# A state-space block with a feed-forward layer on one core: where its tiles lie in SBUF

## The chip, the cores and the metric

One Trainium2 chip, one of its cores. The time is microseconds of device time for one execution of the whole program. Five engines matter here: TensorE (PE; its weight loads are listed apart as PEld), VectorE (DVE), ScalarE (ACT), GpSimd (POOL) and SyncE (SP), which issues nearly all DMAs. SBUF is the on-chip memory in which tiles live, 128 partitions wide; a tile has one start address, the same in each partition, and below "address" always means bytes from the start of a partition.

## The reference, cut to what matters

```python
x = A_u                                            # 1 x 2048 x 512
mod = (silu(c) @ w_mod).reshape(1, 6, 1, -1)
sa, ca, ga, sb, cb, gb = (mod[:, i] for i in range(6))
h = layernorm(x) * (1 + ca) + sa
# S4 convolution: a kernel K[d, l] from 512 x 128 complex parameters,
# y = irfft(rfft(h, 2L) * rfft(K, 2L))[:L] + h * Dskip
x = x + ga * s4(h)
h = layernorm(x) * (1 + cb) + sb
r = maximum(h @ w1 + b1, 0) ** 2                   # 512 -> 1792
x = x + gb * (r @ w2 + b2)                         # 1792 -> 512
```

## The kernel before

The program has two halves, and one core runs them one after the other.

The first half, up to about 300 us, is the convolution as a two-stage discrete Fourier transform written as matmuls. The channels go in 8 groups (`NC`) of 64. For each group the layer-normed input is transformed (`u_pieces`: `stage1` and `stage2`), its halves are swapped by two SBUF-to-SBUF DMAs (`swap_piece`, L777), the convolution's kernel is made from tables of exponentials and sines on POOL, ACT and DVE (`kgen_*`, four units of 16 channels a group, `finish`) and transformed with the same two stages, and `product_pieces` multiplies the spectra (L883) and goes one stage back (L892, copied out by L897). `inverse` (L1088) does the last stage. The second half is the feed-forward layer in split float32r products: `split` (L998, L999) makes a rounded high part on ACT and the rest on DVE or POOL, `three` (L1162 to L1166) multiplies by `w1` in a seven-product scheme, `squares` applies the activation, `product2` (L1204 to L1206) multiplies by `w2`, and `scale` and `store` write out.

The order of work on each engine is computed while the program is built: `keep_order` lists the instructions' data dependences, gives each instruction a modelled duration and an urgency from the `HURRY` table, and pins one order per engine. DMAs go out on SP's queue.

What the change touches is where tiles lie. Tiles come from pools that are filled from two sides. From the left, going up, lie the pool `cst` (small constants, `ctile`), then `ua` (`big0`, the 32 KB tile that holds the parameters, later one half of the back-transformed spectra, later the residual rows `x2`), then `ka` (seven 8 KB tiles `xy0` to `xy6` and the 16 KB `t2_sb`). These are called the lower half below. On the right lies `ub` (`big1`, 32 KB, at the very top), and under it `kp`: the constant selector `spread` in slot `mt`, the two 1 KB tiles `ksb`, the tables `k00` and `k01`, and the three factor tiles `k1`, `k2`, `k3`. These are the upper half. Later tiles reuse these slots: the operands `op...` and `opt...` lie in `xy` slots, `t2t` in that of `t2_sb`, `wset`, `w2t`, `more` (and `i2c` before it) and `work` in `k00`/`k01`, `k1`, `k2` and `k3`, and `rw` in that of `big1`.

Each tile takes a whole number of 32-byte slots. A constant of one float, such as `tiny`, or of two, such as `one_row`, therefore takes 32 bytes, and each such slot in `cst` shifts everything of the lower half by 32 bytes:

```python
    tiny = ctile("tiny", [P, 1])
    one_row = ctile("one_row", [P, 2])
```

Within `kp` the first tile asked for has the lowest address, so the order in which the Python code asks for its tiles sets their places. `spread` is asked for before `kf`, `ksb` at L669, the tables at L785 and the factor tiles at L792.

`tiny` is the bias of a Sign activation in `parameters`. `one_row` holds two columns that sum `ident` over its four quarters; two DVE instructions (L655, L656) read them as per-partition scalars.

Three layouts within tiles come up in the prediction. `piece` and `product_piece` step through an `xy` tile in runs of 16 floats, 64 bytes. `x2`, the residual rows in `big0`, has runs of 64 bytes too. The amplitude tiles in `kgen_rl` (L863) have runs of 32 floats, 128 bytes, every 384 bytes.

Of the kernel before, what the change touches and what calls it, by code (L numbers as in the profile page):

```python
# [39 lines left out]
NE = len(E_VALUES)  # L40
NCH = 64
# [314 lines left out]
def tile_adaln_ssm_ffn(  # L356
# [19 lines left out]
    P = 128  # L376
# [10 lines left out]
    def ring(pool, tag, bufs, shape, dt=F32):  # L387

        if tag not in rings:
            rings[tag] = [[pool.tile(shape, dt, name=f"{tag}{i}") for i in range(bufs)], -1]  # L390
        r = rings[tag]
        r[1] += 1
        return r[0][r[1] % bufs]
# [14 lines left out]
    ctile = lambda name, shape, dt=F32: cst.tile(shape, dt, tag=name, name=name)  # L408
# [6 lines left out]
    unmagic = ctile("unmagic", [P, 1])  # L415
    epsb = ctile("epsb", [P, 1])
    halfpi = ctile("halfpi", [P, 1])
    tiny = ctile("tiny", [P, 1])
    cin = ctile("cin", [P, 4])
    ds4 = ctile("ds4", [P, 128])  # L420
    mv1 = ctile("mv1", [P, 16, 2])
# [5 lines left out]
    def held(pool, slot, name, shape, dt=F32):  # L427

        t = pool.tile(shape, dt, tag=slot, name=name)
        slots[t.tensor.name] = slot  # L430
        return t
# [5 lines left out]
    kp = tc.alloc_tile_pool(name="kp", bufs=1, side="right")  # L437
# [9 lines left out]

    def spectrum():
        return spectra.pop(0)

    def runs(xs):
        return xs.rearrange("p d m t -> p (d m t)")
# [12 lines left out]
    def load_parameters(c0, n):  # L465
        nc.sync.dma_start(raw[:, c0 : c0 + n, 0:6], prm[:, c0 : c0 + n])

    heads = [spectrum() for _ in range(4)]
    rows = [runs(t)[:, 512 * i : 512 * i + 512] for t in heads for i in range(4)]
    load_parameters(0, 1)  # L470
# [11 lines left out]
    def wm_next():  # L482
        wms.append(spectrum())
        wm = wms[-1].rearrange("p a b c -> p (a b c)").rearrange("p (a b) -> p a b", a=4)
        wm_load(wm, len(wms) - 1)
        return wm
# [10 lines left out]
    nc.sync.dma_start(ds4, dskip)  # L497
    make_identity(nc, ident)
    by_q = ident.rearrange("p (q a) -> p q a", q=4)
    one_row = ctile("one_row", [P, 2])  # L500
    nc.vector.tensor_reduce(one_row, by_q[:, :, 0:2].rearrange("p q a -> p a q"), axis=mybir.AxisListType.X, op=ALU.add)
    spread = held(kp, "mt", "spread", [P, 128], FR)
    nc.vector.tensor_tensor(
# [162 lines left out]


    whole, in_turn = {}, set()
    scaled = [ring(kp, "ksb", 2, [P, 4, 64]).rearrange("p d x -> p (d x)") for _ in range(2)]  # L669

    def row_pieces():
        for k in range(8):
# [91 lines left out]
    def u_pieces(c):  # L764
        xs = xus[c] = spectrum()
        for g in range(4):
            stage1(x_sb[c][:, 4 * g : 4 * g + 4], xs, 4 * g, evacuate("u", 4 * c + g))
            yield
        for g in range(4):
            evacuate("w", 4 * c + g)(piece(xs, g), stage2(xs, g))  # L770
            yield
# [10 lines left out]
    AHEAD = 1  # L782


    tables = [held(kp, f"k0{i}", f"tables{i}", [P, 2, NCH * NE]) for i in range(2)]  # L785

    def column(t, x):

        o, n, i = (256, 8, 7 - x) if x < 8 else (0, 4, x - 8) if x < 12 else (768, 16, x - 12)
        return t[..., o : o + 64 * n].rearrange("p c (d x) -> p c d x", d=NCH)[..., i]  # L790

    factors = [held(kp, f"k{i}", n, [P, w]) for i, n, w in ((1, "rtl", 3072), (2, "llph", 4096), (3, "rtlph", 4096))]  # L792
    amps = [t[:, 0:3072].rearrange("p (r d x) -> p r d x", r=2, d=16) for t in factors]
    phs = [t[:, 3072:4096] for t in factors[:0:-1]]

# [471 lines left out]
    for k in (0, 2):  # L1267
# [70 lines left out]
        n = uses.index((k + 1, NF - 2))  # L1338
# [38 lines left out]
def build(arrays):  # L1377
    import concourse.bacc as bacc

    nc = bacc.Bacc("TRN2", target_bir_lowering=False, num_devices=1, dynamic_dma_scratch_size=1024)  # L1380
    args = [nc.dram_tensor(n, a.shape, mybir.dt.from_np(a.dtype), kind="ExternalInput").ap() for n, a in arrays.items()]
    args.append(nc.dram_tensor("out_0_dram", (64, 32, 512), F32, kind="ExternalOutput").ap())
    with tile.TileContext(nc, schedule_with_timeline_sim=True) as tc:
        tile_adaln_ssm_ffn(tc, *args)
    return nc
# [12 lines left out]
```

## Time and profile before

| what | value |
|---|---|
| median of 3 runs | 622.15 us |
| the three runs | 621.27, 622.15, 626.71 us |
| time of the profiled execution | 626.13 us |
| its span, first to last instruction | 624.0 us |
| instructions in the profile | 21112 |
| mean granted TensorE clock | 0.982 |
| DMA moved | 57.00 MB, mean 91 GB/s |

The span is what the profile's views divide up; the 2.1 us around it are launch and end. Busy times are sums over an engine's instructions, so engines overlap. In the list of groups each row is a source line, an engine, an operation, the tile written and those read (their numbers left out), the shapes, the count, the busy time and the mean of one. The view of one source line gives the minimum, median and maximum of one instruction in ns, and for a DMA the time from issue to landing in us.

### The profile page before, as it was taken

What the parts mean: (1) busy time and instruction counts of PE and PEld (TensorE: products, weight loads), DVE (VectorE), ACT (ScalarE), POOL (GpSimd) and SP (SyncE); (2) the same over time, 40 slices, a digit from 0 to 9 for tenths busy, and PEclk for the clock granted to TensorE, in tenths of its full rate; (3) what the DMA queues carried; (4) which work ended last, traced back from release to release, by engine and by line L of the source; (5) the groups of instructions that cost most, each with busy time, mean ns of one, the idle gap of its engine ahead of it and who ended that gap; (6) DMA issues with size and microseconds to landing.
All of it is one profiled execution on the core that took longest, in us unless ns stands there. A gap on an engine that the chain in (4) does not pass through costs nothing.

```text
span 624.0 us, 21112 instructions
## 1 busy us (share of the span) xinstructions
PE 565.9 (91%) x9238; PEld 482.1 (77%) x9238; DVE 494.7 (79%) x870; ACT 419.2 (67%) x747; POOL 246.7 (40%) x202
## 2 busy tenths in 40 slices
PE   1258998999999899997799999999999999999996
PEld 1235988899899899986577778787888877778785
DVE  6898988999999899745798997547999876654744
ACT  5688779979967577443576766665766666666540
POOL 5549998999998789270004100000001300000000
PEclk9969999999999999999799999999999999999999
DMA  8905133030311302357008031113522432111431
GB/s 319 409 3 173 37 71 70 4 70 5 70 30 45 70 5 59 99 147 231 4 15 291 19 118 35 34 35 113 176 83 74 146 102 70 36 33 43 142 101 69
DMA packets 31355, 57.00 MB, mean 91 GB/s; under 512 B 4512, under 2 KB 13600, under 8 KB 29856
## 3 DMA queue, kind: packets, MB, share of 16 engines
q1 hardware_dynamic: 30976, 55.53, 29.5%
q8 instruction: 72, 1.18, 0.8%
q14 instruction: 19, 0.16, 0.1%
q10 hardware_dynamic: 288, 0.13, 0.1%
HBM read 43.07 MB, written 4.19 MB: 76 GB/s over the span
## 4 chain that ended last, share of the span: by engine, by line
PE 61%; DVE 17%; ACT 11%; issue 5%; DMA 3%; POOL 1%; DVEq 0%; SPq 0%; ACTq 0%; POOLq 0%
PE ps L892 7%; PE ps L737 6%; PE ps L747 6%; PE kg L873 4%; PE ps L1162 3%; PE ps L1166 3%; PE ps L1164 3%; PE tg L1204 3%; PE tg L1206 3%; PE tg L1205 3%; PE ps L1204 2%; PE ps L1205 2%; PE ps L1206 2%; ACT tables L820 2%; PE tg L1088 2%
## 5 line engine op out<-in xcount | busy, mean ns | idle before, releaser
L1025 POOL TENSOR_TENSOR work<-work 128x256 f32<-128x256 f32 x4 | 3.4, 850 | 199.6 <-DVE t2t L1156 135.7
L999 DVE TENSOR_TENSOR w2t<-rw,w2t 128x512 fp32r<-128x512 f32 x53 | 37.9, 717 | 42.0 <-ACT w2t L998 41.8
L747 PE MATMUL ps<-xy,t_sb 128*64 128x64 f32 x2048 | 65.8, 223 | 1.0 <-DVE xy L883 1.0
L998 ACT CAST w2t<-rw 128x512 fp32r<-128x512 f32 x53 | 32.8, 620 | 48.7 <-PE kg L1206 25.7
L747 PEld LDWEIGHTS ps<-xy,t_sb 128*64 128x64 f32 x2048 | 63.3, 138 | 2.4 <-DVE xy L883 1.2
L892 PE MATMUL ps<-e_sb,xy 128*64 128x128 f32 x1024 | 60.8, 274 | 1.9 <-DVE xy L883 1.2
L892 PEld LDWEIGHTS ps<-e_sb,xy 128*64 128x64 f32 x1024 | 56.1, 138 | 3.2 <-DVE xy L883 1.4
L1149 ACT ACTIVATE more<-more,b1c 128x512 f32<-128x512 f32 x54 | 38.9, 721 | 25.8 <-DVE more L1187 15.9
L1204 PE MATMUL tg<-w2t,t2t 128*128 128x512 f32 x112 | 44.6, 398 | 0.4 <-DVE t2t L1156 0.4
L1206 PE MATMUL tg<-w2t,t2t 128*128 128x512 f32 x112 | 44.3, 396 | 0.0
L1205 PE MATMUL tg<-w2t,t2t 128*128 128x512 f32 x112 | 44.3, 395 | 0.0
L883 DVE TENSOR_TENSOR xy<-ps,xy 128x512 f32<-128x512 f32 x64 | 39.9, 681 | 0.6 <-PE ps L747 0.4
L998 ACT CAST wset<-work 128x512 fp32r<-128x512 f32 (+2 forms) x36 | 24.6, 689 | 22.3 <-DMA work<-w 15.5
L737 PE MATMUL ps<-d_sb,ksb 128*64 128x128 f32 x512 | 33.7, 275 | 3.5 <-issue 2.2
L829 POOL TENSOR_TENSOR rtlph<-lo,big 128x1024 int32<-128x1024 int32 x16 | 34.7, 2168 | 3.0 <-ACT tg L841 2.5
L829 POOL TENSOR_TENSOR llph<-lo,big 128x1024 int32<-128x1024 int32 x16 | 34.3, 2144 | 3.8 <-ACT tg L841 3.6
L1162 PE MATMUL ps<-opt,wset 128*128 128x512 f32 x84 | 33.8, 402 | 1.2 <-ACT more L1173 1.2
L1204 PE MATMUL ps<-w2t,t2t 128*128 128x512 f32 x84 | 33.9, 403 | 0.0
L1205 PE MATMUL ps<-w2t,t2t 128*128 128x512 f32 x84 | 33.2, 396 | 0.0
L1206 PE MATMUL ps<-w2t,t2t 128*128 128x512 f32 x84 | 33.2, 395 | 0.0
L1164 PE MATMUL ps<-opt,wset 128*128 128x512 f32 x84 | 33.1, 394 | 0.0
L737 PE MATMUL ps<-d_sb,big 128*64 128x128 f32 x512 | 32.1, 274 | 0.3 <-ACT big L697 0.2
(287 smaller groups left out, 1637.4 us busy)
## 6 DMA issues: line engine op xcount, KB each, us to landing
rw<-w SPq DMA_DIRECT2D x53, 256.0 KB, 2.7
xy<-xy SPq DMA_DIRECT2D x16, 512.0 KB, 6.3
xy<-xt SPq DMA_DIRECT2D x24, 256.0 KB, 5.2
xy<-w_mod SPq DMA_DIRECT2D x6, 1024.0 KB, 6.4
work<-w SPq DMA_DIRECT2D x12, 512.0 KB, 4.1
out_dram<-more SPq DMA_DIRECT2D x14, 256.0 KB, 2.0
t_sb<-c_t SPq DMA_DIRECT2D x1, 2048.0 KB, 14.8
i2c<-c_i SPq DMA_DIRECT2D x2, 1024.0 KB, 5.2
```

Of the source, the lines that this page charges most:

```text
L737: nc.tensor.matmul(ps[64 * r : 64 * r + 64, 128 * i : 128 * i + 128], src[:, i], d1_sb[:, r], start=True, stop=True)
L747: nc.tensor.matmul(ps[64 * r : 64 * r + 64, 64 * i : 64 * i + 64].rearrange("p (h q t) -> p q h t", h=2, t=2), t2_sb[:, 8 * g + i, r], src ...
L829: nc.gpsimd.tensor_tensor(ph.rearrange("p d r (a b) -> p (d r) a b", a=4), bc(low_phase[:, us].rearrange("p d r b -> p (d r) b"), 2, 4), b ...
L883: nc.vector.tensor_mul(product_piece(y, g), ps, piece(x, g))
L892: nc.tensor.matmul(ps[64 * m : 64 * m + 64, 128 * i : 128 * i + 128], pairs(y)[:, g, i // 2, 64 * m : 64 * m + 64, i % 2], e1_sb[:, h], st ...
L998: nc.scalar.copy(hi_, raw_)
L1149: nc.scalar.activation(c, c if src is None else src, AF.Relu, bias=b1c[:, t : t + 1])
L1162: pe.append(nc.tensor.matmul(ps, dst[:, 0, wi, kt], o[:, 0, kt], start=start and kt == 0, stop=False, skip_group_check=on))
L1164: pe.append(nc.tensor.matmul(ps, dst[:, 1, wi, kt], o[:, 0, kt], start=False, stop=False, skip_group_check=on))
L1204: nc.tensor.matmul(to[m], l[:, xs], hi_, start=(t == 0), stop=False),
L1205: nc.tensor.matmul(to[m], h[:, xs], lo_, start=False, stop=False),
L1206: nc.tensor.matmul(to[m], h[:, xs], hi_, start=False, stop=(t == NF - 1))])
```

## The change

`tiny` becomes a tile of four floats, and `one_row` becomes two of its columns, where it had been a tile of its own. Sixteen bytes still fit into one 32-byte slot, so `cst` has one slot less. The requests for the tables, the factor tiles and the two `ksb` tiles move up to a place ahead of everything else in `kp`. No computing instruction is added, removed or given another shape.

```diff
-    tiny = ctile("tiny", [P, 1])
+    tiny_and_row = ctile("tiny", [P, 4])
+    tiny, one_row = tiny_and_row[:, 0:1], tiny_and_row[:, 1:3]
...
+    tables = [held(kp, f"k0{i}", f"tables{i}", [P, 2, NCH * NE]) for i in range(2)]
+    factors = [held(kp, f"k{i}", n, [P, w]) for i, n, w in ((1, "rtl", 3072), (2, "llph", 4096), (3, "rtlph", 4096))]
+    scaled = [ring(kp, "ksb", 2, [P, 4, 64]).rearrange("p d x -> p (d x)") for _ in range(2)]
...
-    one_row = ctile("one_row", [P, 2])
...
-    scaled = [ring(kp, "ksb", 2, [P, 4, 64]).rearrange("p d x -> p (d x)") for _ in range(2)]
...
-    tables = [held(kp, f"k0{i}", f"tables{i}", [P, 2, NCH * NE]) for i in range(2)]
...
-    factors = [held(kp, f"k{i}", n, [P, w]) for i, n, w in ((1, "rtl", 3072), (2, "llph", 4096), (3, "rtlph", 4096))]
```

The start addresses in the two built programs:

| tile (and who has its slot later) | before | modulo 512 | after | modulo 512 |
|---|---|---|---|---|
| `d1_sb`, `e1_sb`, `ident` | 1152, 2176, 3200 | 128 | the same | 128 |
| `srep`, `gs4`, `g4`, `s4` | 4992 to 6528 | 384 | 32 lower | 352 |
| `lo` | 7680 | 0 | 7648 | 480 |
| `big0` | 11776 | 0 | 11744 | 480 |
| `xy0` to `xy6` (`op...`, `opt...`) | 44544 to 93696 | 0 | 44512 to 93664 | 480 |
| `t2_sb` (`t2t`) | 101888 | 0 | 101856 | 480 |
| `tables0`, `tables1` (`wset0`, `wset1`) | 122848, 137184 | 480 | 120288, 134624 | 480 |
| `rtl`, `llph`, `rtlph` (`w2t`, `i2c`/`more`, `work`) | 151520, 163808, 180192 | 480 | 2560 lower | 480 |
| `ksb0`, `ksb1` | 120800, 121824 | 480 | 194016, 195040 | 480 |
| `spread` (slot `mt`) | 120288 | 480 | 196064 | 480 |
| `big1` (`rw`) | 196576 | 480 | 196576 | 480 |

So the upper half's tiles change places by multiples of 512 bytes, and the lower half's start 32 bytes lower: from a multiple of 512 (and of 64) to 480 modulo 512, which is 224 modulo 256 and 32 modulo 64.

The order of instructions on PE, DVE, ACT, POOL and SP is the same row for row, with the same waits; only names differ. On DVE the rows around the two readers of `one_row`, after the first modulation rows are multiplied, stand before the change as follows (`s` and `s_parts` are the shift row and its rounded part, `big` is `big0`, the numbers behind the names are tiles).

```order
L653 CAST s_parts<-s_306 128x128
L654 TENSOR_TENSOR s_306<-s_306,s_parts 128x128
L655 TENSOR_SCALAR s_306<-s_306,one_row 128x128
L656 SCALAR_TENSOR_TENSOR s_parts<-s_parts,one_row,s_306 128x128
L587 TENSOR_SCALAR big_83<-big_83 128x7x64 x2
```

And after it, on the same engine at the same place:

```order
L657 CAST s_parts<-s_312 128x128
L658 TENSOR_TENSOR s_312<-s_312,s_parts 128x128
L659 TENSOR_SCALAR s_312<-s_312,tiny 128x128
L660 SCALAR_TENSOR_TENSOR s_parts<-s_parts,tiny,s_312 128x128
L591 TENSOR_SCALAR big_83<-big_83 128x7x64 x2
```

Nothing moved: the lines are four lower and `one_row` is now called by the tile that it lies in.

## The prediction

> **What bounds the kernel now.** I read the page first (busy times, the granted clock, the chain of work that ended last), then the groups by shape, then single source lines for the spread of one instruction, then the DMAs' landing times. On the page: the engines' busy shares, the TensorE clock in 40 slices, and the chain by engine.
>
> ```profile
> PE 565.9 (91%) x9238; PEld 482.1 (77%) x9238; DVE 494.7 (79%) x870; ACT 419.2 (67%) x747; POOL 246.7 (40%) x202
> ...
> PEclk9969999999999999999799999999999999999999
> ...
> PE 61%; DVE 17%; ACT 11%; issue 5%; DMA 3%; POOL 1%; DVEq 0%; SPq 0%; ACTq 0%; POOLq 0%
> ```
>
> PE is busy for 91% of the span and holds 61% of the chain; DVE and ACT hold 28% between them, in the places where PE waits for an eviction or a split. DMA holds 3%. In two slices, the third and the twentieth, the clock was below full. The busy time by stretches shows the second of these (columns: stretch, its length, busy time and count of PE, PEld, DVE, ACT and POOL, clock, DMA share, GB/s):
>
> ```profile
> 296.00:304.00 8.00, 5.68 (x171) 4.28 (x171) 4.89 (x17) 2.28 (x5) 0.00 (x0) 0.50 0.02 4
> ```
>
> For at least these 8 us PE ran at half clock, though not full of work. That matters for reading the runs: 5.68 us of PE work at half clock would be 2.84 us at full clock, so a run without this stretch may be some 3 us shorter with the same program. I take this as the likeliest reason, not shown here, why the three runs lie at 621.27, 622.15 and 626.71 us, and the profiled one at 626.13 us, 3.98 above the median.
>
> **What the change removes and adds.** Instructions: none. The order on every engine and every wait is the same, so a cost can only come from an instruction or a transfer that takes another time at another address. The upper half's tiles move by multiples of 512 bytes; the lower half's by 32. So I look for twins: two groups of one shape, one of which before already has the operands' residues modulo 512 that the other will have. The price of an address is then the difference of the two.
>
> *PE.* The first-stage matmul L737 takes weights from `ksb` (480) and streams `d1_sb` (128). L892 takes weights from `xy` (0) and streams `e1_sb` (128). After the change L892 has exactly L737's residues. In the feed-forward layer L1204 to L1206 take weights from `t2t` (0) and stream `w2t` (480), while L1162 to L1166 take them from `wset` (480) and stream `op`/`opt` (0); after, both have 480 on both sides. In the groups by shape:
>
> ```profile
> L892 PE MATMUL ps<-e_sb,xy 128*64 128x128 f32 x1024 | 60.8, 274 | 1.9 <-DVE xy L883 1.2 <-ACT xy L739 0.7
> L892 PEld LDWEIGHTS ps<-e_sb,xy 128*64 128x64 f32 x1024 | 56.1, 138 | 3.2 <-DVE xy L883 1.4 <-ACT xy L739 0.9
> ...
> L1206 PE MATMUL tg<-w2t,t2t 128*128 128x512 f32 x112 | 44.3, 396 | 0.0
> ...
> L737 PE MATMUL ps<-d_sb,ksb 128*64 128x128 f32 x512 | 33.7, 275 | 3.5 <-issue 2.2 <-ACT tg L839 0.8 <-DVE big L897 0.5
> ...
> L1164 PE MATMUL ps<-opt,wset 128*128 128x512 f32 x84 | 33.1, 394 | 0.0
> ...
> L737 PEld LDWEIGHTS ps<-d_sb,ksb 128*64 128x64 f32 x512 | 28.1, 137 | 5.3 <-issue 2.8 <-ACT tg L839 1.0 <-DVE big L897 0.7
> ...
> L1206 PEld LDWEIGHTS tg<-w2t,t2t 128*128 128x128 f32 x112 | 21.0, 188 | 5.1
> ...
> L1164 PEld LDWEIGHTS ps<-opt,wset 128*128 128x128 f32 x84 | 15.8, 188 | 3.4
> ```
>
> 274 against 275, 138 against 137, 396 against 394, 188 against 188 ns: a difference of at most 2 ns, in either direction. The busy time of L892 is 60.8 us for 1024, about 59 ns of PE's time each (274 ns is a latency in a pipeline). One ns on each of the 1024 would be 1.0 us, and that is the bound I carry for L892 from both sides. I take 0, since the twins' weights differ by 1 ns the other way. The second-stage matmuls L747 read `t_sb` and `xy`, both lower, both shifted by the same 32 bytes; they have no twin, and I price them like L892: 0, bound 2.0 us either way (2048 of them).
>
> *DVE and ACT on contiguous tiles.* `split` is the same code on either half:
>
> ```profile
> L739 ACT COPY xy<-ps 128x512 f32<-128x512 f32 x43 | 24.6, 587 | 10.3 <-PE ps L737 10.3
> ...
> L999 DVE TENSOR_TENSOR wset<-work,wset 128x1024 fp32r<-128x1024 f32 x8 | 9.8, 1223 | 3.2 <-ACT wset L998 3.2
> ...
> L999 DVE TENSOR_TENSOR opt<-work,opt 128x1024 fp32r<-128x1024 f32 x8 | 9.6, 1215 | 0.0
> ...
> L697 ACT COPY big<-ps 128x512 f32<-128x512 f32 x16 | 8.9, 587 | 1.9 <-PE ps L691 1.8
> ...
> L999 DVE TENSOR_TENSOR op<-work,op 128x512 fp32r<-128x512 f32 x12 | 7.8, 685 | 0.7 <-ACT op L998 0.7
> ...
> L998 ACT CAST wset<-work 128x512 fp32r<-128x512 f32 x12 | 7.4, 621 | 15.5 <-DMA work<-w 15.5
> ...
> L998 ACT CAST op<-work 128x512 fp32r<-128x512 f32 x12 | 7.0, 622 | 0.1
> ...
> L999 DVE TENSOR_TENSOR wset<-work,wset 128x512 fp32r<-128x512 f32 x8 | 5.5, 686 | 1.8 <-ACT wset L998 1.8
> ```
>
> `op` and `opt` lie low (0) and `work` high (480): mixed residues. `wset` and `work` are both at 480, as all will be. 685 and 686, 1215 and 1223, 622 and 621; and 587 for copies into the lower `xy` and the upper `big1`. With the 8 ns of the 1024 pair as the bound, the 16 mixed instructions here change by 0.1 us. I take 0.
>
> *DVE, ACT and PE on runs of 64 bytes.* L883, L770 and all that works on `x2` step through lower tiles in 64-byte runs that begin at multiples of 64 before, and at 32 modulo 64 after. There is no exact twin. The nearest row is L863, which reads and writes 128-byte runs in upper tiles that begin at 32 modulo 64 (480 + 384 d). A third row is L897, whose 64 copies write 16-byte runs, half into `big0` (0), half into `big1` (480); 38 are on DVE, from both halves. Minimum, median and maximum of one, in ns:
>
> ```profile
> L883 DVE TENSOR_TENSOR xy<-ps,xy x64: 678/680/692, 92.7 to 278.2; 128x512 f32<-128x512 f32 x64
> ...
> L863 DVE SCALAR_TENSOR_TENSOR rtl<-rtl,tg x11: 674/677/687, 53.3 to 245.8; 128x512 f32<-128x512 f32 x11
> ...
> L897 DVE COPY big<-ps x38: 410/415/425, 104.7 to 285.5; 128x256 f32<-128x256 f32 x38
> ```
>
> Runs that begin at 32 modulo 64 cost L863 nothing against L883's aligned ones (677 and 680), nor do 64-byte runs cost L883 anything against the contiguous 685. L897 has one narrow band of 15 ns, with no second group. I take 0. As the upper bound, let each run cost one element more: (1215 - 685) / 512 = 1.04 ns. L883 has 32 runs in and 32 out, 67 ns, times 64 is 4.3 us of DVE; at DVE's 17% of the chain, 0.7 us of the time. Below, nothing: a run cannot be cheaper than the contiguous row shows.
>
> *DMA.* Loads into `xy`, `big0` and `t2_sb` and the swaps now end on addresses at 224 modulo 256. Twins are the loads into upper tiles, which have lain so all along. From the views of single lines (L987 and L478 go to lower tiles, L1043 and L981 to upper ones), and from the waits the one in which PE waits for a lower load:
>
> ```profile
> L987 SPq DMA_DIRECT2D xy<-xt x8: 328/424/987, 277.7 to 281.9; - x8
> ...
> DMA to landing us min/median/max: 2.5/3.9/5.1
> ```
>
> ```profile
> L1043 SPq DMA_DIRECT2D rw<-w x53: 327/328/505, 327.0 to 606.3; - x53
> ...
> DMA to landing us min/median/max: 2.5/2.7/6.2
> ```
>
> ```profile
> L478 SPq DMA_DIRECT2D xy<-w_mod x6: 368/373/379, 14.1 to 59.2; - x6
> ...
> DMA to landing us min/median/max: 4.9/6.4/11.2
> ```
>
> ```profile
> L981 SPq DMA_DIRECT2D i2c<-c_i x2: 327/336/346, 273.6 to 291.5; - x2
> ...
> DMA to landing us min/median/max: 5.1/5.2/5.2
> ```
>
> ```profile
> PE ps L628 <- DMA xy<-w_mod: 1.6, 2, 1.1
> ```
>
> Unqueued, a 256 KB load lands in 2.5 us in either half; a 1 MB load in 4.9 us low and 5.1 us high. So the price is between 0 and 0.2 us a megabyte, and it counts where someone waits: 1.6 us in two waits of PE for `w_mod`. Two loads late by 0.2 us each make 0.4. I take 0.2 us. The swaps L777 shift at both ends, but nothing on DVE is listed as waiting for them.
>
> [...]
>
> *The two readers of `one_row`* and the bias `tiny` read the same number of bytes on the same engines as before: 0.
>
> **The sum:** 0 (PE) + 0 (splits) + 0 (runs) + 0.2 (DMA) = +0.2 us. On the profiled execution 626.13 + 0.2 = 626.3; on the median 622.15 + 0.2 = 622.35, say 622.3 us. The measurement moves by more than this by itself: the three runs span 5.4 us.
>
> **The rivals.**
>
> *Slower, by runs that straddle.* Place: L883 and its kin. If a 64-byte run at 32 modulo 64 cost k elements more, the 4.3 us of DVE become 4.3 k, and the path gets 17% of it, 0.7 k. From k = 9 the kernel is 1% (6.2 us) slower, 628.5 us or more. For it speaks that no row shows just this form; against it, L863's 677 ns. Chance 0.08.
>
> *Slower within 1%, by DMA.* With the price of 0.2 us a megabyte on every lower load, and waits that are hidden now coming up, 1 to 3 us: 624 us. For it speaks that 5.1 is above 4.9 and that PE already waits for `w_mod`; against it the 256 KB twins. Chance 0.10. [...]
>
> *Faster, by equal residues.* If instructions whose operands mix residues paid now, equal residues would give it back. To be 1% faster, 6.2 us, each of 1024 L892 matmuls would have to gain 6 ns of PE's time, to 616 us. The twins differ by 1 or 2 ns. Chance 0.07, most of it for a gain in L747, which has no twin.
>
> **How the numbers follow.** No change but the sum has 0.75. A measurement of this kernel tells about 1% from no change, from 615.9 to 628.4 us. Within it lie the forecast, the DMA rival, and most of what remains, together 0.85. Faster by more takes 0.07 from its rival, slower 0.08. The range: 2.0 + 1.0 us of the PE bounds below the forecast, 619.3, and above it the 626.71 of the upper run with the 0.7 of the runs' bound, 627.4. Rounded, 619.0 to 627.5.
>
> **What would show it.** In the profile after, L892 near 274 and 138 ns, L883 near 680, L747's busy time at its old value, L628's wait for `w_mod` below 2.5 us, and the means of the twins above where they are. A time near 626 with a half-clock stretch at 296 us, and one near 622 without, would both be this forecast. It would be wrong if L883 went above 700 ns, if PE's weight loads from the lower half grew, or if the first stage's loads pushed out the start of L691.

## The result, and the profile after

| | before | after |
|---|---|---|
| median | 623.72 us (19 runs, 621.27 to 626.71) | 619.38 us (19 runs, 616.54 to 623.25) |
| ratio, 95% interval | | 0.9931, 0.9912 to 0.9951 |
| profiled execution, its span | 626.13 us, 624.0 us | 618.05 us, 615.9 us |

The kernel became 4.3 us faster, 0.7%. That lies inside the forecast range and within the 1% named as "about no change", but the interval ends below 1, so the change does something, and the forecast was 0.2 us more, which is nothing that a measurement could tell.

From the page of the kernel after, the engines' busy shares, the granted clock and the chain:

```profile
PE 562.8 (91%) x9238; PEld 483.9 (79%) x9238; DVE 494.7 (80%) x870; ACT 418.6 (68%) x747; POOL 246.1 (40%) x202
...
PEclk9999999999999999999699999999999999999999
...
PE 59%; DVE 19%; ACT 12%; issue 4%; DMA 4%; POOL 2%; DVEq 0%; ACTq 0%; SPq 0%; POOLq 0%
```

PE is busy for 3.1 us less (565.9 before) and holds 59% of the chain instead of 61%; DVE's 494.7 us is the same, and one slice instead of two shows less than the full clock. The groups by shape of the kernel after say which instructions of PE:

```profile
L750 PE MATMUL ps<-xy,t_sb 128*64 128x64 f32 x2048 | 66.0, 223 | 1.0 <-DVE xy L884 1.0
...
L893 PE MATMUL ps<-e_sb,xy 128*64 128x128 f32 x1024 | 60.8, 274 | 1.9 <-DVE xy L884 1.2 <-ACT xy L742 0.7
...
L1207 PE MATMUL tg<-w2t,t2t 128*128 128x512 f32 x112 | 43.6, 390 | 0.0
...
L740 PE MATMUL ps<-d_sb,ksb 128*64 128x128 f32 x512 | 33.8, 276 | 3.6 <-issue 2.3 <-ACT tg L840 0.8 <-DVE big L898 0.5
...
L1165 PE MATMUL ps<-opt,wset 128*128 128x512 f32 x84 | 32.8, 391 | 0.0
...
L742 ACT COPY xy<-ps 128x512 f32<-128x512 f32 x43 | 24.6, 586 | 10.5 <-PE ps L740 10.4
...
L1000 DVE TENSOR_TENSOR op<-work,op 128x512 fp32r<-128x512 f32 x12 | 7.8, 687 | 0.7 <-ACT op L999 0.7
```

The first half's matmuls (L893, L740), the copies and the splits stand where they were (274, 276, 586, 687 against 274, 275, 587, 685 ns). The matmuls of the feed-forward layer are shorter: the second product has 390 ns where it had 396 (L1207, L1206 before), the first 391 where it had 394 (L1165, L1164 before). Such small differences of means could be a few outliers. The view of the single line, with minimum, median and maximum, shows that they are not. Before:

```profile
L1206 PE MATMUL tg<-w2t,t2t x112: 395/396/397, 328.7 to 582.1; 128*128 128x512 f32 x112
```

And after:

```profile
L1207 PE MATMUL tg<-w2t,t2t x112: 387/390/396, 325.7 to 575.1; 128*128 128x512 f32 x112
```

The whole group has moved: the median is 6 ns shorter, and the longest now is as long as the old median. The durations overlap: in the 40 us below lie 172 matmuls of about 396 ns, 68 us in sum. So the pace is read from the windows (columns as in the prediction: stretch, length, busy time and count of PE, PEld, DVE, ACT, POOL, clock, DMA share, GB/s). Of the kernel before, the first loads, the feed-forward layer from the first `ps<-op,wset` of L1166 to the last `kg<-w2t,t2t` of L1206, and 40 us in which PE works without a gap, on the second product for most of the time (124 of the 171 matmuls that start in it) and on the first for the rest:

```profile
5.00:30.00 25.00, 6.58 (x104) 5.32 (x104) 20.42 (x55) 17.23 (x84) 14.33 (x16) 1.00 1.06 412
...
312.70:618.50 305.80, 304.06 (x1672) 242.52 (x1671) 228.02 (x368) 194.84 (x321) 17.63 (x14) 1.00 0.28 86
...
560.00:600.00 40.00, 40.00 (x172) 32.01 (x172) 23.45 (x37) 21.59 (x37) 0.00 (x0) 1.00 0.31 92
```

The same of the kernel after, and the stretch at half clock:

```profile
5.00:30.00 25.00, 7.54 (x104) 6.18 (x104) 20.45 (x55) 17.25 (x84) 14.31 (x16) 1.00 1.06 396
...
296.00:304.00 8.00, 7.33 (x210) 5.80 (x209) 7.37 (x25) 3.74 (x7) 0.00 (x0) 0.50 0.03 5
...
309.80:610.40 300.60, 297.83 (x1672) 242.47 (x1671) 228.09 (x368) 194.17 (x321) 17.23 (x14) 1.00 0.28 87
...
560.00:600.00 40.00, 39.99 (x177) 32.80 (x176) 24.03 (x38) 19.05 (x34) 0.00 (x0) 1.00 0.32 100
```

At full clock, without a gap, 40 us hold 177 matmuls where they held 172: one every 226 ns instead of every 233 ns. The layer takes 300.6 us instead of 305.8, 5.2 us less, with the same 1672 matmuls. PE's busy time in it fell by 6.2 us and its idle time rose from 1.7 to 2.8 us. From the waits of the kernel after, the one that grew most in the layer, and the two that are put down to the loads of `w_mod`:

```profile
PE ps L1163 <- ACT more L1174: 1.9, 3, 0.9
...
PE ps L632 <- DMA xy<-w_mod: 1.6, 2, 0.9
```

PE waits longer for ACT's evictions in the first product, 1.9 us where the kernel before has 1.2 for this wait. The two waits put down to `w_mod` come to 1.6 us as before; a longer wait ahead of them is read further down, under the prediction's DMA term.

The two spans differ by 8.1 us: 5.2 in the layer, 2.9 ahead of it, and nothing behind it (5.5 us from the last such matmul to the end in both). The 2.9 us belong to these two executions: in the kernels below the layer starts between 309.5 and 313.0 us, the latest with the lower half at 480 (`e1_low_only`), the earliest with it at 0 (`h1_w1_only`).

### The profile page after: what moved, and what is told of

It is laid out like the page before. It is cut to its first block, busy times and chain, and to the rows that moved or that the text cites. A ratio compares the mean times of both kernels' runs of the same rounds, so it can differ in the third digit from the quotient of the medians.

```text
span 615.9 us, 21112 instructions
## 1 busy us (share of the span) xinstructions
PE 562.8 (91%) x9238; PEld 483.9 (79%) x9238; DVE 494.7 (80%) x870; ACT 418.6 (68%) x747; POOL 246.1 (40%) x202
## 4 chain that ended last, share of the span: by engine, by line
PE 59%; DVE 19%; ACT 12%; issue 4%; DMA 4%; POOL 2%; DVEq 0%; ACTq 0%; SPq 0%; POOLq 0%
PE ps L893 7%; PE ps L740 7%; PE ps L750 6%; PE ps L1163 4%; PE kg L874 3%; PE ps L1165 3%; PE ps L1167 3%; PE tg L1205 3%; PE tg L1206 3%; PE tg L1207 3%; DMA work<-w 2%; PE ps L1207 2%; PE ps L1205 2%; PE ps L1206 2%; ACT tables L821 2%
## 5 line engine op out<-in xcount | busy, mean ns | idle before, releaser
L750 PE MATMUL ps<-xy,t_sb 128*64 128x64 f32 x2048 | 66.0, 223 | 1.0 <-DVE xy L884 1.0
L750 PEld LDWEIGHTS ps<-xy,t_sb 128*64 128x64 f32 x2048 | 63.4, 138 | 2.5 <-DVE xy L884 1.2
L893 PE MATMUL ps<-e_sb,xy 128*64 128x128 f32 x1024 | 60.8, 274 | 1.9 <-DVE xy L884 1.2
L893 PEld LDWEIGHTS ps<-e_sb,xy 128*64 128x64 f32 x1024 | 56.1, 139 | 3.2 <-DVE xy L884 1.4
L1205 PE MATMUL tg<-w2t,t2t 128*128 128x512 f32 x112 | 44.0, 393 | 0.6 <-DVE t2t L1157 0.6
L1206 PE MATMUL tg<-w2t,t2t 128*128 128x512 f32 x112 | 43.7, 390 | 0.0
L1207 PE MATMUL tg<-w2t,t2t 128*128 128x512 f32 x112 | 43.6, 390 | 0.0
L884 DVE TENSOR_TENSOR xy<-ps,xy 128x512 f32<-128x512 f32 x64 | 39.9, 683 | 0.7 <-PE ps L750 0.6
L740 PE MATMUL ps<-d_sb,ksb 128*64 128x128 f32 x512 | 33.8, 276 | 3.6 <-issue 2.3
L1163 PE MATMUL ps<-opt,wset 128*128 128x512 f32 x84 | 34.0, 404 | 1.9 <-ACT more L1174 1.9
L1205 PE MATMUL ps<-w2t,t2t 128*128 128x512 f32 x84 | 33.5, 398 | 0.0
L1207 PE MATMUL ps<-w2t,t2t 128*128 128x512 f32 x84 | 32.9, 391 | 0.0
L1165 PE MATMUL ps<-opt,wset 128*128 128x512 f32 x84 | 32.8, 391 | 0.0
L1206 PE MATMUL ps<-w2t,t2t 128*128 128x512 f32 x84 | 32.8, 390 | 0.0
L740 PE MATMUL ps<-d_sb,big 128*64 128x128 f32 x512 | 32.1, 274 | 0.3 <-ACT big L700 0.2
## 6 DMA issues: line engine op xcount, KB each, us to landing
t_sb<-c_t SPq DMA_DIRECT2D x1, 2048.0 KB, 15.4
```

Source lines behind the costliest of these rows:

```text
L740: nc.tensor.matmul(ps[64 * r : 64 * r + 64, 128 * i : 128 * i + 128], src[:, i], d1_sb[:, r], start=True, stop=True)
L750: nc.tensor.matmul(ps[64 * r : 64 * r + 64, 64 * i : 64 * i + 64].rearrange("p (h q t) -> p q h t", h=2, t=2), t2_sb[:, 8 * g + i, r], src ...
L884: nc.vector.tensor_mul(product_piece(y, g), ps, piece(x, g))
L893: nc.tensor.matmul(ps[64 * m : 64 * m + 64, 128 * i : 128 * i + 128], pairs(y)[:, g, i // 2, 64 * m : 64 * m + 64, i % 2], e1_sb[:, h], st ...
L1163: pe.append(nc.tensor.matmul(ps, dst[:, 0, wi, kt], o[:, 0, kt], start=start and kt == 0, stop=False, skip_group_check=on))
L1165: pe.append(nc.tensor.matmul(ps, dst[:, 1, wi, kt], o[:, 0, kt], start=False, stop=False, skip_group_check=on))
```

## The experiments

The theories. **A**: a matmul in float32r goes faster when its weights and its streamed operand begin at equal residues (the first form: modulo 512; A64 and A128: equality modulo 64 or 128 is enough). **B**: what counts is that the lower half begins at 32 modulo 64, whatever the other operand. **C**: what counts is the new order of the upper half. **D**: the difference is one of executions and chips. In all kernels the order of the computing instructions is that of before. All start from the kernel before, whose lower half is at 0 and whose upper half is at 480, modulo 512.

### One part of the change alone, and equality at another residue

`e1_low_only` has the shared slot and not the new order of requests:

```diff
-    tiny = ctile("tiny", [P, 1])
+    tiny_and_row = ctile("tiny", [P, 4])
+    tiny, one_row = tiny_and_row[:, 0:1], tiny_and_row[:, 1:3]
...
-    one_row = ctile("one_row", [P, 2])
```

> Only the shared slot: the lower half moves to 480 modulo 512, the upper half stays at the addresses of before. Theory A (weights and streamed operand of a float32r matmul read faster when their start addresses have the same residue modulo 512): the matmuls of the feed-forward layer have a mean of 389 to 392 ns, and the time is 0.993 of before (619 us). Theory B (rows that start at 32 modulo 64 read faster than rows at a multiple of 64): the same, 0.993. Theory C (the gain comes from the new places of the upper half): means of 394 to 398 ns and 1.000 of before. Theory D (no matmul is faster, the gain is another run's clock and waits): 1.000.

`e2_up_only` has the new order of requests and not the shared slot, so that the lower half stays at 0:

```diff
+    tables = [held(kp, f"k0{i}", f"tables{i}", [P, 2, NCH * NE]) for i in range(2)]
+    factors = [held(kp, f"k{i}", n, [P, w]) for i, n, w in ((1, "rtl", 3072), (2, "llph", 4096), (3, "rtlph", 4096))]
+    scaled = [ring(kp, "ksb", 2, [P, 4, 64]).rearrange("p d x -> p (d x)") for _ in range(2)]
...
-    scaled = [ring(kp, "ksb", 2, [P, 4, 64]).rearrange("p d x -> p (d x)") for _ in range(2)]
...
-    tables = [held(kp, f"k0{i}", f"tables{i}", [P, 2, NCH * NE]) for i in range(2)]
...
-    factors = [held(kp, f"k{i}", n, [P, w]) for i, n, w in ((1, "rtl", 3072), (2, "llph", 4096), (3, "rtlph", 4096))]
```

> Only the earlier requests: the upper half takes its new places, the lower half stays at multiples of 512. Theories A and B: matmul means of 394 to 398 ns and 1.000 of before. Theory C: 389 to 392 ns and 0.993. Theory D: 1.000.

`e3_all_zero` is the kernel before with 480 bytes of padding under `big1`, so that the upper half begins at 0 too:

```diff
+    ub.tile([P, 120], F32, tag="pad", name="pad")
```

> 480 bytes of padding at the top put the upper half at multiples of 512 too, so both halves have residue 0. Theory A: matmul means of 389 to 392 ns and 0.993 of before, since the residues are equal. Theory B: 394 ns or more and 1.000 to 1.01, since now both rows start at a multiple of 64. Theory C gives no number of its own, the upper half has yet other places. Theory D: 1.000.

Measured against 624.62 us on the same chip: `e1_low_only` 619.58 us, ratio 0.9917 (0.9884 to 0.9950); `e2_up_only` 625.26 us, 1.0002 (0.9977 to 1.0028); `e3_all_zero` 618.74 us, 0.9905 (0.9869 to 0.9940). The pace, in the windows of `e1_low_only`:

```profile
560.00:600.00 40.00, 39.98 (x177) 32.66 (x176) 23.84 (x38) 20.83 (x36) 0.00 (x0) 1.00 0.31 93
```

of `e2_up_only`, with its layer:

```profile
312.80:617.40 304.60, 303.76 (x1673) 242.42 (x1671) 227.95 (x367) 194.21 (x320) 17.23 (x14) 1.00 0.28 86
...
560.00:600.00 40.00, 40.00 (x173) 32.01 (x172) 23.47 (x38) 22.07 (x37) 0.00 (x0) 1.00 0.28 92
```

and of `e3_all_zero`, with its first loads and its layer:

```profile
5.00:30.00 25.00, 6.99 (x104) 5.51 (x104) 20.44 (x55) 17.21 (x84) 14.32 (x16) 0.99 1.05 412
...
311.00:611.00 300.00, 297.77 (x1672) 242.25 (x1672) 227.83 (x368) 194.22 (x321) 17.17 (x14) 1.00 0.29 87
...
560.00:600.00 40.00, 39.99 (x177) 32.79 (x176) 24.03 (x38) 19.61 (x34) 0.00 (x0) 1.00 0.33 99
```

177, 173 and 177: the shared slot does it, the new order does nothing (C falls), and it is not the 32 modulo 64 either, since `e3_all_zero` has the lower half at 0, as before, and is as fast (B falls). Two kernels whose edits have no line in common, both faster by an interval that excludes 1, leave nothing for D.

### A residue for each operand

`s1_sweep` pads the `xy` tiles so that the seven operands of the first product lie at 0, 32, 64, 128, 256, 384 and 480 modulo 512, with `wset` at 480, and names them by it (`zerod`, `onee`, `twob`, `threec`, `fourf`, `fiveg`, `sixa` in this order). `t2t` comes to 480.

```diff
-    spectra = [held(ka, f"xy{i}", f"xy{i}", [P, 4, 128, 4]) for i in range(XY)]
+    spectra = []
+    for i in range(XY):
+        if (0, 8, 8, 16, 32, 32, 24)[i]:
+            ka.tile([P, (0, 8, 8, 16, 32, 32, 24)[i]], F32, tag=f"pad{i}", name=f"pad{i}")
+        spectra.append(held(ka, f"xy{i}", f"xy{i}", [P, 4, 128, 4]))
```

> The weights (wset) stay at 480 modulo 512; padding between the lower tiles gives each streamed operand a residue of its own: opzerod 0, oponee 32, optwob 64, opthreec 128, opfourf 256, opfiveg 384, opsixa 480; t2t lies at 480 as w2t does. Theory A: only opsixa and the products with t2t have a mean of 389 to 392 ns, all others 394 to 398. Theory B: oponee too has 389 to 392, as every row at 32 modulo 64. Theory C: all stay at 394 to 398.

One run, 620.29 us. From the groups by shape of `s1_sweep`, the first product's third line (L1170), and from the views of single lines (minimum, median and maximum) its first line (L1166) for the operand at 480:

```profile
L1170 PE MATMUL ps<-opfiveg,wset 128*128 128x512 f32 x28 | 8.9, 400 | 0.0
L1170 PE MATMUL ps<-opfourf,wset 128*128 128x512 f32 x28 | 8.8, 395 | 0.0
L1170 PE MATMUL ps<-oponee,wset 128*128 128x512 f32 x28 | 8.7, 391 | 0.0
L1170 PE MATMUL ps<-opsixa,wset 128*128 128x512 f32 x28 | 8.6, 390 | 0.0
L1170 PE MATMUL ps<-optwob,wset 128*128 128x512 f32 x24 | 7.7, 401 | 0.0
...
L1166 PE MATMUL ps<-opsixa,wset x28: 389/393/712, 310.0 to 557.1; 128*128 128x512 f32 x28
```

On the third line the operand at 480 has the 390 ns of the fast kernels, and the mean goes up to 401 ns at 64. But the operand at 32 has 391 ns there, and on the first line the operand at 480 has a median of 393 ns, hardly less than the 394 of the one at 32. (The mean there is 408 ns, which two of the 28 make, the longer with 712 ns: a reason to look at medians.) In most of the runs of six matmuls on the operand at 480 the first three take 392 to 395 ns and the last three 389, so the place within the run counts too, and why is not shown. Theory A's expectation, that only the operand at 480 would lie at 389 to 392 ns, is not met as it was put. So the sweep says that the price depends on the residue, and not which residues are equal. Moving everything together does.

### The whole lower half at 32, 96 and 224

`l64`, `l128` and `l256` add a constant of 8, 24 or 56 floats to `cst` (this is `l64`):

```diff
+    ctile("pad", [P, 8])
```

The lower half then begins at 32, 96 and 224 modulo 512. From the 480 of the upper half that is 64 or 128 bytes up, past the next multiple of 512, and 256 bytes down.

> The lower half lies 32 bytes higher than before, at 32 modulo 512, 64 above the upper half's 480; both halves then start at 32 modulo 64. Theory A as stated (equal modulo 512): means of 394 to 398 ns in both products. Its variant A64 (a difference of a multiple of 64 is enough): 389 to 392.

> The lower half at 96 modulo 512, 128 above the upper half's 480. Theory A: 394 to 398 ns. Variant A64: 389 to 392. Variant A128 (a multiple of 128 is enough): 389 to 392 here and not at a difference of 64.

> The lower half at 224 modulo 512, 256 from the upper half's 480. Theory A: 394 to 398 ns. Variants A64, A128 and A256: 389 to 392.

One run each: 624.39, 624.17 and 618.37 us, where the kernel before has a median of 622.94 us on this chip. The windows of `l128`, then of `l256`:

```profile
5.00:30.00 25.00, 7.55 (x104) 6.18 (x104) 20.44 (x55) 17.23 (x84) 14.31 (x16) 1.00 1.06 397
...
560.00:600.00 40.00, 40.00 (x173) 32.25 (x172) 23.26 (x37) 21.53 (x37) 0.00 (x0) 1.00 0.29 89
```

```profile
5.00:30.00 25.00, 7.85 (x104) 6.18 (x104) 20.43 (x55) 17.24 (x84) 14.32 (x16) 1.00 1.06 396
...
560.00:600.00 40.00, 39.99 (x177) 32.79 (x176) 24.01 (x38) 19.31 (x34) 0.00 (x0) 1.00 0.32 99
```

`l64` has 173 as well. Distances of 64 and 128 are slow, so A64 and A128 fall, and `l64`, which lies at 32 modulo 64, is a second witness against B. A distance of 256 is as fast as 0. The 480 on both sides that the change makes is one case among these: of the distances tried, 0 and 256 are fast (177 in 40 us), and 32, 64 and 128 are not (172 or 173).

### One product at a time

`h1_w1_only` moves `wset` to 0, with the tables that have its slots before it, which makes the first product's pair equal (0 and 0) and leaves the second's (0 and 480). The pads stand ahead of and behind the tables:

```diff
+    kp.tile([P, 8], F32, tag="pada", name="pada")
     tables = [held(kp, f"k0{i}", f"tables{i}", [P, 2, NCH * NE]) for i in range(2)]
+    kp.tile([P, 120], F32, tag="padb", name="padb")
```

> Only the two tiles of w1's parts (wset, and the tables before them) move to residue 0, where the lower half lies as before; w2t stays at 480. Theory A (equal residues of weights and streamed operand): the 588 matmuls of the first product fall to means of 389 to 392 ns, the 672 of the second stay at 394 to 398, and the time falls by about 588/1260 of what equal residues on both gave (0.8 to 0.95%), so to 0.995 to 0.996 of before. A rival (the place of the lower half alone matters, whatever the weights): nothing changes, 1.000.

`h2_w2_only` moves `t2t` to 480, with `t_sb`, which has its slot before it, which makes the second product's pair equal and leaves the first's:

```diff
+    ka.tile([P, 120], F32, tag="padt", name="padt")
```

> Only the tile of t_sb and t2t moves, by 480 bytes of padding, to 480, where w2t lies; the other lower tiles stay at 0. Theory A: the 672 matmuls of the second product fall to 389 to 392 ns, the 588 of the first stay at 394 to 398; 672 times 6.0 ns are 4.0 us, so 0.993 to 0.995 of before. A rival (what counts is where all lower tiles lie, not the pair): no change, 1.000.

`h12_pairs` has the pads of both:

```diff
+    ka.tile([P, 120], F32, tag="padt", name="padt")
...
+    kp.tile([P, 8], F32, tag="pada", name="pada")
     tables = [held(kp, f"k0{i}", f"tables{i}", [P, 2, NCH * NE]) for i in range(2)]
+    kp.tile([P, 120], F32, tag="padb", name="padb")
```

> Both pairs equal, but not all tiles: wset and the operands at 0, w2t and t2t at 480. Theory A, told by pairs: all 1260 matmuls at 389 to 392 ns and 0.990 to 0.993 of before. If tables at residue 0 cost something in the first half, as the unchanged time with wset alone suggests, 0.993 to 0.997.

`h3_tables_only` puts only the tables of the first half, which share a slot with `wset`, at 0, and leaves `wset` at 480:

```diff
-    tables = [held(kp, f"k0{i}", f"tables{i}", [P, 2, NCH * NE]) for i in range(2)]
+    wide = [held(kp, f"k0{i}", f"tables{i}", [P, 3712]) for i in range(2)]
+    tables = [t[:, 8:3592].rearrange("p (c x) -> p c x", c=2) for t in wide]
```

> The tables start 32 bytes into their slots, at residue 0, and wset at 480 as before: of the kernel with wset and the tables moved, only the tables' part. No float32r matmul changes (394 to 398 ns). If the tables' residue took back what the first product had gained: 1.003 to 1.005 of before. If it did not (the first product's PE time is covered by other engines in most runs, or the interval was unlucky): 1.000.

Measured: `h1_w1_only` 622.40 us against 622.94, ratio 1.0001 (0.9980 to 1.0022), which misses the expected 0.995 to 0.996. Against 625.24 us on another chip `h2_w2_only` 620.34 us, 0.9930 (0.9904 to 0.9955); `h12_pairs` 620.53 us, 0.9927 (0.9900 to 0.9954); `h3_tables_only` 624.27 us, 1.0003 (0.9973 to 1.0033). The groups of `h1_w1_only`, one of each product:

```profile
L1208 PE MATMUL tg<-w2t,t2t 128*128 128x512 f32 x112 | 44.3, 396 | 0.0
...
L1168 PE MATMUL ps<-opt,wset 128*128 128x512 f32 x84 | 26.0, 391 | 0.0
```

and the same of `h2_w2_only`:

```profile
L1207 PE MATMUL tg<-w2t,t2t 128*128 128x512 f32 x112 | 43.7, 390 | 0.0
...
L1167 PE MATMUL ps<-opt,wset 128*128 128x512 f32 x84 | 26.4, 395 | 0.0
```

396 and 391 in the one, 390 and 395 in the other: each product goes by its own pair, and no common start of all tiles is needed. The layer in the windows of `h1_w1_only`:

```profile
309.50:612.80 303.30, 301.75 (x1672) 242.43 (x1671) 228.15 (x368) 194.32 (x321) 17.53 (x14) 1.00 0.28 86
```

of `h2_w2_only`:

```profile
311.10:612.60 301.50, 300.35 (x1672) 242.25 (x1671) 227.29 (x367) 193.72 (x320) 17.41 (x14) 1.00 0.28 87
```

of `h12_pairs`:

```profile
311.60:612.70 301.10, 298.75 (x1673) 242.43 (x1671) 228.14 (x368) 194.15 (x321) 17.34 (x14) 1.00 0.28 87
```

and of `h3_tables_only`:

```profile
312.00:616.10 304.10, 303.56 (x1673) 242.21 (x1671) 227.81 (x367) 194.08 (x320) 17.38 (x14) 1.00 0.28 86
```

Three kernels with unequal pairs in both products (before, `e2_up_only`, `h3_tables_only`) have layers of 305.8, 304.6 and 304.1 us, mean 304.8, with PE busy for 304.1, 303.8 and 303.6 us, mean 303.8. This shows what one profile can tell: the layer to 1 or 2 us. Against these means:

| pairs made equal | PE busy in the layer | length of the layer | ratio of times |
|---|---|---|---|
| first product (`h1_w1_only`) | -2.0 us | -1.5 us | 1.0001 |
| second product (`h2_w2_only`) | -3.4 us | -3.3 us | 0.9930 |
| both (`h12_pairs`) | -5.0 us | -3.7 us | 0.9927 |
| both (the change itself) | -6.0 us | -4.2 us | 0.9931 |
| both (`e3_all_zero`) | -6.0 us | -4.8 us | 0.9905 |

The second product passes its gain on. When both are faster, PE saves 1.6 to 2.6 us more and the layer gains 0.4 to 1.5 us more; the rest is idle time, most of it PE's wait for ACT's evictions in the first product (L1163 above), 1.0 us in `h2_w2_only`, 1.8 in `h12_pairs` and 1.9 after the change. How much the first product gains alone stays open: the profile says 1.5 us, no more than the three kernels with unequal pairs differ among themselves, and the interval of the times ends at 0.9980, 1.2 us. One way out would be that the tables at 0 cost the first half what the first product gains. `h3_tables_only` shows no sign of it, but does not rule it out: its interval reaches 1.0033, 2.1 us.

### Equal residues in the first half too

In the first half L747 reads two lower tiles. They have equal residues in most kernels, but not in `h2_w2_only` and `h12_pairs`, where `t_sb` lies at 480 and `xy` at 0: there L747 holds 66.0 and 65.7 us of PE, for 65.8 before the change and 66.0 after it. L737 and L892 have had equal residues in no kernel so far, since `d1_sb` and `e1_sb` stay at 128. `v1_constants_too` merges the slots as the change does and pads the constants so that `d1_sb`, `e1_sb` and `ident` and the whole lower half lie at 224 modulo 512, with the upper half at 480: all are equal modulo 256. It was also a candidate for a version faster than the change.

```diff
+    ctile("pada", [P, 24])
...
-    tiny = ctile("tiny", [P, 1])
+    tiny_and_row = ctile("tiny", [P, 4])
+    tiny, one_row = tiny_and_row[:, 0:1], tiny_and_row[:, 1:3]
...
+    ctile("pad", [P, 40])
...
-    one_row = ctile("one_row", [P, 2])
```

> All large tiles at equal residues modulo 256, and 96 bytes of padding ahead of them put the two small matrices of the first stages (d1_sb, e1_sb) there too, so that the float32 matmuls of the first half also read two operands of equal residue. If the rule holds for them: the 1024 back-stage matmuls on e1_sb fall below their 60.8 us of busy time by 2% or more (as the float32r ones did), and the time goes to 0.985 to 0.990 of before. If it holds for float32r matmuls with 128 x 128 weights alone: 60.7 to 61.0 us as in every kernel so far, and 0.991 to 0.994.

619.77 us against 624.12, ratio 0.9926 (0.9899 to 0.9953), like the change itself. From the groups of `v1_constants_too`:

```profile
L894 PE MATMUL ps<-e_sb,xy 128*64 128x128 f32 x1024 | 60.7, 274 | 1.9 <-DVE xy L885 1.2 <-ACT xy L741 0.7
...
L739 PE MATMUL ps<-d_sb,ksb 128*64 128x128 f32 x512 | 33.7, 276 | 3.4 <-issue 1.7 <-ACT tg L841 1.2 <-DVE big L899 0.5
```

274 and 276 ns, as with unequal residues. What was found holds for the float32r matmuls with 512 streamed columns, and not for these float32 ones with 128, nor for L747's with 64. Whether the number type or the number of columns makes the difference was not tried.

## Why the prediction was wrong, though the time lies in its range

**PE: the step that failed.** The argument for 0 in the feed-forward layer was a pair of twins: L1206 (`t2t` 0, `w2t` 480) with 396 ns and L1164 (`wset` 480, `op` 0) with 394 ns. It was read as "another residue of the weights costs nothing". But both twins have unequal residues, 0 and 480, and after the change both operands have 480, which no float32r group of the kernel before had. Two rows that agree show only that what differs between them costs nothing, and what the change makes new, two equal residues, was in neither. The term measured: the median matmul of the layer's 1260 takes 390 ns instead of 396, PE's busy time there falls by 6.0 us against the three kernels with unequal pairs (4.8 ns a matmul), and the layer by some 4.2 us, beside 4.3 us between the medians of the times. Of the signs that the prediction named, "the means of the twins where they are" is the one that did not hold.

**The range.** That 619.38 us lies in 619.0 to 627.5 is luck. The 3.0 us below the forecast were bounds of 1.0 and 2.0 us on L892 and L747, which hold 60.8 and 66.0 us after the change for 60.8 and 65.8 before. The layer that did gain 4.2 us had been given no bound. And the kernel before has a median of 623.72 us over 19 runs, 1.6 us above the 622.15 of the three from which the range was counted.

**The rival "faster, by equal residues"** had what made the kernel faster, and by chance the 6 ns a matmul, but in the wrong place: on L892, which hasn't moved in any kernel, not even with equal residues (`v1_constants_too`). Its chance of 0.07 came from twins that could not speak about it. The gain in L747, on which most of that chance lay, did not come: as L750 it holds 66.0 us of PE for 65.8 before. It could not come from equal residues, since both its operands lie in the lower half and were equal already.

**DVE, ACT, and runs of 64 bytes.** 0 was right. L883, now L884, is at 682 ns (680), and L897's copies, now L898, at 417 ns (415). From the views of single lines after:

```profile
L884 DVE TENSOR_TENSOR xy<-ps,xy x64: 680/682/697, 92.7 to 276.7; 128x512 f32<-128x512 f32 x64
...
L898 DVE COPY big<-ps x38: 414/417/426, 104.6 to 283.9; 128x256 f32<-128x256 f32 x38
```

The rival of runs that straddle, which needed nine elements a run, got at most 2 ns of the 67 that one element a run would have cost.

**DMA.** The term was 0.2 us, from a price of 0 to 0.2 us a megabyte. In the trace the first three loads of `w_mod`, 1 MB each and one behind the other, land 2.48 and 2.55 us apart before and 2.71 and 2.74 us after. So the upper end of the price was about right: 0.2 us a megabyte, 9% and 8%. The twins could not show it: of a 256 KB load 9% is 0.06 us, and the fastest of the eight loads of that size at L987 takes 2.5 to 2.9 us in the seven profiles that write it to 0 and 2.5 to 3.0 us in the six that write it to 32, 96, 224 or 480.

Two things were left out. The price adds up along a queue: after all the loads ahead of it the first of these three lands at 22.8 us instead of 21.6, and the third at 28.2 instead of 26.6. And PE does wait for them. From the waits before, after, and in `h1_w1_only`:

```profile
PE ps L628 <- DVE big L550: 13.8, 1, 13.8
```

```profile
PE ps L632 <- DVE st L616: 15.0, 1, 15.0
```

```profile
PE ps L628 <- DMA xy<-w_mod: 15.2, 3, 14.0
```

The prediction counted 1.6 us in two waits for `w_mod` and left the 13.8 us ahead of them to DVE. But in all fourteen profiles PE's first modulation matmul starts 0.13 to 0.14 us after the first of these loads has landed, and in `h1_w1_only` the same wait is put down to the load. (A wait for several things is put down to the one that came last by the profile, which need not be the one that counted.) So PE's waits there grew from 15.4 to 16.6 us, more than the term. It is made up for soon after: L691, whose start the prediction named as a sign, begins at 40.9 us in both kernels.

Over the first loads' stretch, 5 to 30 us, 412 GB/s became 396. This goes with the lower half's start and not with the matmuls: 412 to 415 GB/s in the seven profiles of kernels that start it at 0 (before, `e2_up_only`, `e3_all_zero` and the four of the section on single products, in two of which `t_sb` alone lies at 480), 394 to 397 in the six that start it at 32, 96, 224 or 480 (after, `e1_low_only`, `l64`, `l128`, `l256`, `v1_constants_too`). That is 4% less; `s1_sweep`, whose tiles have mixed residues, lies between with 406. The starts at 32, 96 and 480 do not differ among themselves: in `l64` (32) and `l128` (96) the first two loads of `w_mod` land as far apart as after the change (480), 2.71 us.

**The spread of the runs.** The half-clock stretch near 296 us was to tell runs near 622 from runs near 626. The profiled execution of the kernel after has such a stretch (0.50, 296 to 304 us) and took 618.05 us, below the median, and each of the fourteen profiles has one that begins between 290 and 295 us. So it does not part them, and what does is open.

## What to carry to other kernels

Where a float32r matmul of 128 x 128 weights and 512 columns sets the pace, try the weights and the streamed operand at starts that are equal modulo 256: here that gave 177 matmuls in 40 us instead of 172 or 173, and it cost a pad of 32 to 480 bytes and no other change. The matmuls' pace went by pair here (390 ns in the second product and 395 in the first with only the second's pair equal), so each pair can be mended by itself; what reaches the time depends on what else that stage waits for (ratio 0.9930 for the second pair alone, 1.0001 for the first). When a price is taken from twins, first write down which relation between the operands the change makes new, and look whether either twin has it; if none has, the bound comes from the pace that the group could have, not from their agreement. A pace that is 3% faster in 40 us without a gap came to 2% of PE's busy time in the layer (6.2 of 304.1 us) and 0.7% of the kernel's time, since the layer is half of it and part of the gain became waiting for the evictions. And before a wait is left out of a term, compare when it ends with when the transfer lands, whatever name the profile gives it.

## What the runs showed of the hardware

- In these runs the start addresses of the two operands of the float32r matmuls (128 x 128 weights, 512 columns) matter together: one every 226 or 227 ns (177 or 176 in 40 us) with a distance of 0 or 256 modulo 512, one every 231 to 233 ns (172 or 173 in 40 us) with the distances of 32, 64 and 128 modulo 256 that were tried. Which residues they are made no difference among those tried: 0 and 0 (`e3_all_zero`), 480 and 480 (the change), 224 and 480 (`l256`) have 177 each. The weight loads last 188 ns in either case (L1206 before, L1207 after), and the 6 ns a matmul are no listed wait: the idle time before both groups is 0.0 us. What in the chip makes it so was not shown by any run, nor whether the weights that count are the matmul's own or those loaded meanwhile for the next one (before, L1205's load of 0.19 us starts at 587.95 us together with L1204's matmul of 0.40 us, and L1205's own matmul at 588.18): outside the sweep both lie in the same tile.
- In these runs loads from HBM, one behind the other, took 2.71 to 2.76 us a megabyte where the lower half, into which they write, starts at 32, 96, 224 or 480 modulo 512, and 2.47 to 2.57 us where it starts at 0 (the `w_mod` loads); over the first 5 to 30 us that is 394 to 397 GB/s against 412 to 415. `e3_all_zero` has equal residues and its lower half at 0; its ratio, 0.9905, is the lowest, but its interval, 0.9869 to 0.9940, overlaps with that of the change, so it is not shown to be better.
